# Two gate rows of an adaLN block: from wide broadcast matmuls to width-1 column matmuls, spread by DMA through DRAM

## Chip, cores, metric

One core of one Trainium2 chip. The metric is device time in microseconds (us) for one execution; medians of several runs are quoted. The record marks an execution slow when it is over 1.5% above the fastest of its kernel; all runs compared here are fast, except that two looks of one run each (marked) have no state of their own.

## The reference, cut

```python
mod = (_silu(c) @ w_mod).reshape(c.shape[0], 6, 1, -1)      # c: 1x512, w_mod: 512 x 3072
sa, ca, ga, sb, cb, gb = (mod[:, i] for i in range(6))      # six rows of 512
x = x + ga * _A_ref(_layernorm(x) * (1 + ca) + sa, ...)     # attention, 32 heads, 2048 tokens
x = x + gb * _B_ref(_layernorm(x) * (1 + cb) + sb, ...)     # gated MLP mixing over tokens
```

The block is of the adaLN kind: shift, scale and gate of each layer normalisation are rows computed from a vector `c`. `sa, ca, sb, cb` multiply tensors whose feature axis lies on the partitions, so the kernel wants them as columns (128 partitions x 4). `ga` and `gb` multiply tensors with tokens on the partitions, so it wants them as a row of 512 repeated on all 128 partitions.

## The kernel before

It runs 128 attention "units" (8 head groups x 16 token tiles) of eight slots each. Calls hung at `(unit, slot)` are issued at the start of that slot, ahead of its own matmuls. Its matmuls write to tiles in PSUM; the small pieces of work here share two PSUM buffers ("banks") named "misc", which VectorE empties.

```python
def mod_part(i, wmod, w0, mc_ps):          # columns: 16 matmuls of width 1 for one part
    for dt in range(NDT):
        for kt in range(NDT):
            nc.tensor.matmul(mc_ps[:, i * NDT + dt : i * NDT + dt + 1],
                lhsT=wmod[:, kt, w0 + dt * P : w0 + (dt + 1) * P],
                rhs=sc_bf[:, kt : kt + 1], start=(kt == 0), stop=(kt == NDT - 1))
...
def qk(u, i):                              # two width-512 matmuls and one exponential per slot
    ...
def pv(u, i):                              # eight width-129 matmuls per slot
    ...
def wo_proj(u):                            # one width-512 matmul in each of slots 4 to 7,
    ...                                    # reads oT, a DMA transpose of the attention output
...
at(8, 1, lambda: rest_w.update(lhs=mod_lhs()))   # 4 broadcasts of silu(c) to 128x128
at(9, 4, mod_cols_b)                             # sb, cb: mod_part twice
at(10, 4, lambda: mod_row(ga_rows, 2, rest_w["lhs"]))   # 4 matmuls of width 512
at(11, 4, lambda: mod_row(gb_rows, 5, rest_w["lhs"]))
...
at(it + 7, 3, lambda g=g: load_wq(g, nc.gpsimd))        # loads of the next head group
```

## Time and profile before

| | before |
|---|---|
| time, median of 3 runs | 1323.28 us (1322.88 to 1323.29) |
| TensorE share of the chain that ended last | 98% |
| plain attention unit | 8.81 us |
| unit with a gate row (four width-512 matmuls) | 9.67 us |
| unit with 32 width-1 matmuls | 9.61 us |

The lines behind the table are in the prediction. How to read it: TensorE never runs dry in the loop (busy for 57.70 of the 57.70 us from 84.6 to 142.3), so the length of a unit is the sum of what TensorE does in it, and the difference between a unit with and one without some piece of work is what that piece costs.

### The profile page before, as it was taken

How to read it: one execution, taken by the hardware profiler on the slowest of the kernel's cores; microseconds unless marked ns; L12 is line 12 of the kernel's file. 1: busy time of each engine (PE TensorE's matmuls, PEld its weight loads, DVE VectorE, ACT ScalarE, POOL GpSimd, SP SyncE). 2: the span in 40 equal slices, each digit the busy share in tenths (PEclk: the TensorE clock that was granted, in tenths of full speed). 3: DMA queues.
4: the chain of work that ended last, by engine and by line, in shares of the span. 5: the costliest groups of instructions: out<-in, count | busy, mean ns of one | idle time of the engine just before them, and what ended most of it. 6: DMA issues, size and time to landing. Idle time of an engine off the chain costs nothing.

```text
span 1321.5 us, 27879 instructions
## 1 busy us (share of the span) xinstructions
PE 1312.4 (99%) x12335; PEld 858.3 (65%) x12335; DVE 473.5 (36%) x1166; ACT 1077.8 (82%) x1061; POOL 49.4 (4%) x92
## 2 busy tenths in 40 slices
PE   9999999999999999999999999999999999999998
PEld 5666666666666666666666666666666666644445
DVE  5632222222222222222222222222222566794444
ACT  6898999999999999999999999999999999650000
POOL 1200000000000000000000000000000000120000
PEclk9999999999999999999999999999999999999999
DMA  7541022102111112111110211021101111143300
GB/s 180 141 104 33 14 49 37 37 15 51 31 23 35 32 37 37 31 35 37 33 36 14 53 37 33 18 53 21 33 14 21 25 33 30 33 116 80 69 21 26
DMA packets 148704, 58.12 MB, mean 44 GB/s; under 512 B 138368, under 2 KB 144768, under 8 KB 148576
## 3 DMA queue, kind: packets, MB, share of 16 engines
q1 hardware_dynamic: 141776, 37.65, 15.1%
q0 software_dynamic: 4208, 16.39, 4.1%
q10 hardware_dynamic: 2592, 2.23, 0.5%
q8 instruction: 98, 1.61, 0.5%
q14 instruction: 30, 0.25, 0.1%
HBM read 21.37 MB, written 2.10 MB: 18 GB/s over the span
## 4 chain that ended last, share of the span: by engine, by line
PE 98%; DMA 0%; DVE 0%; SPq 0%; issue 0%
PE o_ps L993 35%; PE s_ps L971 33%; PE misc L1025 8%; PE misc L938 8%; PE misc L1344 7%; PE s_ps L1190 2%; PE s_ps L1229 2%; PE o_ps L1365 1%; PE s_ps L1365 1%; DMA x_sb<-in_A_x_dram 0%; PE misc L1101 0%; DVE tmp L1377 0%; DVE yout L1378 0%; DVE bnst L691 0%; SPq L700 0%; SPq L745 0%
## 5 line engine op out<-in xcount | busy, mean ns | idle before, releaser
L978 ACT ACTIVATE pT<-s_ps 128x1024 bf16<-128x1024 f32 x1024 | 1044.5, 1025 | 82.9 <-PE s_ps L971 9.0
L993 PEld LDWEIGHTS <-pT 128*128 128x128 bf16 x8192 | 548.5, 98 | 241.2
L993 PE MATMUL o_ps<-v,pT 128*128 128x129 bf16 x8192 | 631.4, 220 | 0.0
L971 PE MATMUL s_ps<-qT,kT 128*128 128x512 bf16 x2048 | 609.0, 379 | 0.0
L1004 DVE RECIPROCAL rall<-o_ps 128x2 f32<-128x2 f32 x256 | 43.7, 171 | 743.8 <-PE o_ps L993 743.5
L971 PEld LDWEIGHTS <-kT 128*128 128x128 bf16 x2048 | 199.3, 98 | 118.7 <-DVE qT L920 0.5
L1025 PE MATMUL misc<-wo_g,oT 128*128 128x512 bf16 x512 | 194.0, 379 | 0.0
L938 PE MATMUL misc<-hT,wq_g 128*128 128x512 bf16 (+2 forms) x528 | 189.6, 371 | 0.0
L1005 DVE TENSOR_TENSOR onorm<-o_ps,rall 128x256 bf16<-128x256 f32 x256 | 108.7, 425 | 9.0 <-DVE rall L1004 0.3
L1344 PE MATMUL misc<-wsp,z 128*128 128x512 bf16 (+2 forms) x560 | 100.7, 336 | 0.0
L949 DVE CAST qT<-misc 128x512 bf16<-128x512 f32 x127 | 86.3, 681 | 1.8 <-PE misc L938 1.6
L1344 PEld LDWEIGHTS <-z 128*128 128x128 bf16 x560 | 50.6, 98 | 48.5
L1038 DVE TENSOR_TENSOR xacc<-misc,xacc 128x512 f32<-128x512 f32 x112 | 76.2, 680 | 0.0
L938 PEld LDWEIGHTS <-wq_g 128*128 128x128 bf16 x528 | 50.6, 98 | 1.1 <-issue 0.2
L1025 PEld LDWEIGHTS <-oT 128*128 128x128 bf16 x512 | 50.1, 98 | 0.8
L1359 DVE TENSOR_TENSOR gb<-misc,bsp_bc 128x512 bf16<-128x512 f32 (+1 forms) x28 | 18.4, 659 | 59.0 <-PE misc L1344 59.0
L1190 PE MATMUL s_ps<-win_sb,hT 128*128 128x448 bf16 x128 | 27.0, 352 | 0.0
L1200 ACT ACTIVATE z<-s_ps 128x896 bf16<-128x896 f32 x16 | 14.7, 917 | 14.9 <-PE s_ps L1190 14.9
L1229 PE MATMUL s_ps<-hT,win_sb 128*128 128x512 bf16 x112 | 24.5, 379 | 0.0
L1237 ACT ACTIVATE z1T<-s_ps 128x1024 bf16<-128x1024 f32 x14 | 14.3, 1024 | 10.0 <-PE s_ps L1229 9.1
L691 DVE BATCH_NORM_STATS2 bnst<-x_sb 128x6 f32<-128x512 bf16 x32 | 21.9, 684 | 1.5 <-DMA x_sb<-in_A_x_dram 1.0
L715 POOL DMA_DIRECT2D wq_g<-in_A_wq_dram x7 | 5.3, 753 | 420.9 <-PE misc L938 420.9
(87 smaller groups left out, 283.2 us busy)
## 6 DMA issues: line engine op xcount, KB each, us to landing
wq_g<-in_A_wq_dram POOLq DMA_DIRECT2D x7, 512.0 KB, 3.8
v<-in_A_v_cache_dram POOLq DMA_DIRECT2D x7, 512.0 KB, 7.2
wo_g<-in_A_wo_dram POOLq DMA_DIRECT2D x7, 512.0 KB, 4.7
oT<-onorm SPq DMA_TRANSPOSE x128, 2.4
wsp<-in_w_mod_dram POOLq DMA_DIRECT2D x1, 2048.0 KB, 11.7
out_dram<-yout ACTq DMA_DIRECT2D x16, 128.0 KB, 1.7
win_sb<-in_B_w_in_dram POOLq DMA_DIRECT2D x1, 1792.0 KB, 7.7
x_sb<-in_A_x_dram SPq DMA_DIRECT2D x3, 512.0 KB, 5.6
```

What stands on the lines that cost most here:

```text
L938: nc.tensor.matmul(ps[0][:, o0 : o0 + n], lhsT=wqs[g][:, dt, hh * DH : (hh + 1) * DH], rhs=hTs[ch][:, dt, c0 : c0 + n], start=(dt == 0), s ...
L949: nc.vector.tensor_copy(out=dst, in_=src)
L971: nc.tensor.matmul(s_ps[:, h * 512 : (h + 1) * 512].rearrange("p (r q) -> p r q", r=REP), lhsT=groups[g]["kT"][:, kt * P : (kt + 1) * P], ...
L978: nc.scalar.activation(out=pTs[u][:, 2 * i : 2 * i + 2, :], in_=s_ps[:].rearrange("p (k q) -> p k q", k=2), func=ACT.Exp, scale=inv_sqrt_dh,)
L993: nc.tensor.matmul(o_ps[:, hh % 2, 0 : DH + 1], lhsT=pTs[u][:, kt, hh * P : (hh + 1) * P], rhs=groups[g]["v1"][:, kt, 0 : DH + 1], start=( ...
L1004: nc.vector.reciprocal(out=rall[:, c0 : c0 + 2], in_=o_ps[:, :, DH])
L1005: nc.vector.tensor_tensor(out=onorms[u][:, hh - 1 : hh + 1, :], in0=o_ps[:, :, 0:DH], in1=rall[:, c0 : c0 + 2].unsqueeze(2).to_broadcast([ ...
L1025: nc.tensor.matmul(X_ps[:], lhsT=oTs[u][:, hh, :], rhs=groups[g]["wo"][:, hh, :], start=(hh == 0), stop=(hh == REP - 1),)
L1038: nc.vector.tensor_tensor(out=xaccs[j][:], in0=X_ps[:], in1=xaccs[j][:], op=ALU.add)
L1190: nc.tensor.matmul(ps[0][:, hf * 512 : hf * 512 + FC], lhsT=h2Ts[j // CT][:, dt, (j % CT) * P : (j % CT + 1) * P], rhs=win_sb[:, dt, FH + ...
L1229: nc.tensor.matmul(ps[0][:, k * 512 : (k + 1) * 512], lhsT=win_sb[:, dt, f * P : (f + 1) * P], rhs=h2Ts[2 * ch2 + k][:, dt, :], start=(dt ...
L1344: nc.tensor.matmul(g_ps[:, :n], lhsT=z2[:, st, f * P : (f + 1) * P], rhs=wsp[t][:, st, c0 : c0 + n], start=(st == 0), stop=(st == NT - 1 a ...
```

## The change

Its intent: the wide form computes each gate row 128 times over, once for every partition, in matmuls 512 columns wide (0.86 us for four). The narrow form computes each value once, as columns, and leaves the spreading to DMA, which has time to spare: before the change the DMA engines are busy for 7% and 23% of the two units with gate rows.

```diff
--- before.py
+++ after.py
@@ -635,6 +635,7 @@
     psum = fast.enter_context(
         tc.tile_pool(name="psum", bufs=2, space=bass.MemoryType.PSUM)
     )
+    dram = fast.enter_context(tc.tile_pool(name="dram", bufs=1, space=bass.MemoryType.DRAM))
     res = fast.enter_context(tc.tile_pool(name="res", bufs=1))
     stat = fast.enter_context(tc.tile_pool(name="stat", bufs=2))
     wspp = fast.enter_context(tc.tile_pool(name="wspp", bufs=1, side="right"))
@@ -1079,33 +1080,23 @@
         at(it + 1, 4, second)
         at(it + 2, 5, third)
 
-    def mod_lhs():
-        lhs = []
-        for kt in range(NDT):
-            lhs_bc = res.tile([P, P], BF16, name=f"lhs_bc{kt}")
-            nc.vector.tensor_scalar_mul(
-                out=lhs_bc[:], in0=ones_bf[:], scalar1=sc[:, kt : kt + 1]
-            )
-            lhs.append(lhs_bc)
-        return lhs
-
     def mod_cols_b():
         mc_ps = bank("misc")
         for i in range(2):
             mod_part(i, wmod_b, (1 + i) * D, mc_ps)
         mod_copy(3, mc_ps)
 
-    def mod_row(row_out, i, lhs):
-        mr_ps = bank("misc")
-        for kt in range(NDT):
-            nc.tensor.matmul(
-                mr_ps[:],
-                lhsT=lhs[kt][:],
-                rhs=wmod_b[:, kt, (i - 2) * D : (i - 1) * D],
-                start=(kt == 0),
-                stop=(kt == NDT - 1),
-            )
-        nc.vector.tensor_copy(out=row_out[:], in_=mr_ps[:])
+    def mod_rows():
+
+        mc_ps = bank("misc")
+        for i, row in enumerate((0, 3)):
+            mod_part(i, wmod_b, row * D, mc_ps)
+        for i, (part, rows) in enumerate(((2, ga_rows), (5, gb_rows))):
+            cols = slice(part * NDT, (part + 1) * NDT)
+            nc.vector.tensor_copy(out=modc[:, cols], in_=mc_ps[:, i * NDT : (i + 1) * NDT])
+            line = dram.tile([D], FP32, name=f"mod{part}")
+            nc.gpsimd.dma_start(out=line[:].rearrange("(dt p) -> p dt", p=P), in_=modc[:, cols])
+            nc.gpsimd.dma_start(out=rows[:], in_=line[:].partition_broadcast(P))
 
     def load_wsp(tile_, t, st):
         nc.sync.dma_start_transpose(
@@ -1146,13 +1137,10 @@
     ln1_at(1, (0, 7), (1, 2), (2, 2))
     ln1_at(2, (2, 4), (3, 1), (4, 5))
     ln1_at(3, (5, 1), (5, 5), (7, 4))
-    rest_w = {}
     at(2, 5, lambda: nc.gpsimd.dma_start(out=wmod_b, in_=wmod_dram[:, :, 2 * D : NMOD]))
     at(5, 5, lambda: nc.gpsimd.dma_start(out=win_sb[:], in_=win_dram))
-    at(8, 1, lambda: rest_w.update(lhs=mod_lhs()))
     at(9, 4, mod_cols_b)
-    at(10, 4, lambda: mod_row(ga_rows, 2, rest_w["lhs"]))
-    at(11, 4, lambda: mod_row(gb_rows, 5, rest_w["lhs"]))
+    at(10, 4, mod_rows)
 
     def set_fill(b):
 
```

## The prediction

> **What bounds the kernel now.** I read the page from the coarse parts to the fine ones: engine shares, the chain that ended last, then that chain in time around the instructions that the change touches.
>
> ```profile
> PE 1312.4 (99%) x12335; PEld 858.3 (65%) x12335; DVE 473.5 (36%) x1166; ACT 1077.8 (82%) x1061; POOL 49.4 (4%) x92
> ...
> PE 98%; DMA 0%; DVE 0%; SPq 0%; issue 0%
> PE o_ps L993 35%; PE s_ps L971 33%; PE misc L1025 8%; PE misc L938 8%; PE misc L1344 7%; PE s_ps L1190 2%; PE s_ps L1229 2%; PE o_ps L1365 1%; PE s_ps L1365 1%; DMA x_sb<-in_A_x_dram 0%; PE misc L1101 0%; DVE tmp L1377 0%; DVE yout L1378 0%; DVE bnst L691 0%; SPq L700 0%; SPq L745 0%
> ```
>
> TensorE is busy 99% of the span, and 98% of the chain is TensorE as well: almost nothing ever makes it wait. So a change pays what it takes off or puts on TensorE's own stream, and work on other engines counts only if it creates a wait that is not there today. The matmuls to be replaced (line 1101) are in the chain, at a rounded 0%. That alone says that the size is small. Closer:
>
> ```profile
> 94.63 0.78 PE misc L848 x32
> 95.41 0.45 PE s_ps L971 x2
> ```
>
> ```profile
> 104.24 0.86 PE misc L1101 x4
> ```
>
> ```profile
> 113.91 0.86 PE misc L1101 x4
> ```
>
> Columns are start, length (both us), what. Line 1101 is the two gate rows, four matmuls of width 512 each, one group in attention unit 10 and one in unit 11. Line 848 is the form that the change goes over to: 32 matmuls of width 1, here for the shift and scale columns sb and cb in unit 9, from the same weight tile. So the kernel before already holds a measurement of the new form, in the same place of the loop (slot 4 of a unit).
>
> A check by another route is the period of the loop. The first output-projection matmul of each unit starts at these times:
>
> ```profile
> 86.71 0.22 PE misc L1025
> ...
> 96.32 0.22 PE misc L1025
> ```
>
> ```profile
> 105.99 0.22 PE misc L1025
> ```
>
> ```profile
> 115.66 0.22 PE misc L1025
> ```
>
> ```profile
> 124.46 0.21 PE misc L1025
> ```
>
> ```profile
> 133.27 0.22 PE misc L1025
> ```
>
> The periods are 9.61, 9.67, 9.67, 8.80 and 8.81 us. The plain unit takes 8.81; the unit with 32 narrow matmuls takes 0.80 more, each unit with a gate row 0.86 more. These marginal costs hold any start-up or switching cost that the lengths of pieces could miss, and they agree with them within 0.02 us.
>
> [...] the line 1101 matmuls are recorded at 379 ns each, while four of them advance the chain by only 0.86 us, 215 ns each. I therefore count in chain time and periods, not in recorded durations.
>
> [...] 0.86/4 = 215 ns, and 0.78/32 = 24.4 ns. [...] a width-1 matmul needs its own 128x128 weight load, recorded at 96 ns. [...] 32 loads lie within 1.06 us before and beside the group, 33 ns apart, so several are in flight together.
>
> [...] The trace has 1.7 us for the 1 KB load of c (issued elsewhere) and 3.8 us for 512 KB of wq[...].
>
> **The change part by part.**
>
> TensorE, removed: two groups of four width-512 matmuls, 2 x 0.86 = 1.72 us of the chain. Added: 32 width-1 matmuls (two parts x four output blocks x four contraction blocks) as one group in unit 10, 0.80 us by the period of unit 9 (0.78 by piece). Net on TensorE: 0.80 - 1.72 = -0.92 us.
>
> VectorE, removed: four broadcast multiplies of 128x128 (248 ns each, 0.99 us) and two copies of 128x512 (681 ns each, 1.36 us). Added: two copies of 128x4, at 156 ns by the existing one of that shape, 0.31 us. Net -2.04 us, worth nothing: VectorE is 36% busy and no TensorE wait of this stage is put on it. The PSUM bank of the gates comes free sooner, since 0.31 us of copies stand where 0.68 us stood; also worth nothing, as TensorE did not wait for the bank.
>
> GpSimd queue, added: four DMAs. The order of instructions in the changed build puts them after the loads for head group 1 and ahead of the wq load for group 2. Each write takes 512 single FP32 elements (128 partitions x 4) to DRAM, and each read spreads 2 KB over 128 partitions, 256 KB in all. Estimates from this trace: a 512-piece load costs GpSimd 0.75 (wq) to 0.96 us (w_mod) to issue, a 128-piece broadcast 0.59 us. A landing should take 2 to 4 us for the scattered write and 2 to 6 us for the spread (512 KB of b_sp by broadcast took 5.9). A read waits in the queue for its own write to land, so one pair holds the queue some 0.9 + 3 + 0.6 = 4.5 us and both some 9 us: from 105.4, when the copies end, to about 114.4. What stands around that:
>
> ```profile
> 62.75 0.76 POOL L733 DMA_DIRECT2D wo_g<-in_A_wo_dram  x1
> 114.20 0.75 POOL L715 DMA_DIRECT2D wq_g<-in_A_wq_dram  x1 [50.69 <-PE misc L938]
> 163.05 0.20 POOL L721 MEMSET v<- 128x128 bf16 x1 [48.10 <-PE o_ps L993]
> ```
>
> The queue idles for 50.69 us before the wq load of 114.20 and 48.10 us before the next step. So the four DMAs fall into idle time. The worst case delays that wq load by a few microseconds; the first matmul that reads it starts at 269.77, and it lands in 3.8 us, so it has about 150 us to spare.
>
> Use of the rows: ga_rows is first read at 1036.2, gb_rows at 1221.3; both would be in place by about 120, more than 900 us early.
>
> Sum: 1323.28 - 0.92 = 1322.36, rounded to 1322.4 us.
>
> **The rivals.**
>
> First, narrow matmuls could run at the pace of their weight loads: 32 x 96 ns = 3.07 us instead of 0.80, making the kernel 3.07 - 1.72 = 1.35 us slower, 1324.6. For it: one full weight load per column of output. Against it: the existing group of the same form took 0.78 us, with weights from the same tile.
>
> Second, DMA trouble. The 1,024 four-byte writes and the two spreads could slow the transposes of onorm on the SP queue (2.4 us each), on which the output projection waits. Their slack is large: the projection of a unit runs two iterations after its attention product began, so a transpose issued at the end of one 8.8 us iteration is first read one and a half iterations later, some 13 us. A held-up GpSimd queue has the 150 us above. Only if the queue stood still beyond all of this would time be lost; I would expect 0 to 2 us then.
>
> Third, ScalarE takes over as the bound, and the saving is lost. It is the nearest engine: 8 exponentials of 1025 ns make 8.20 us per unit against TensorE's 8.81. But units without gate rows already run at 8.81 with TensorE gapless, so unit 11 shortened to 8.81 becomes only what its neighbours are. Effect on the time: none.
>
> Fourth, a hopeful one: the shorter VectorE list starts something earlier. With no TensorE wait on VectorE here, there is nothing to gain; the kernel stays at 1322.4.
>
> **Range and chances.** The effect is 0.07% of the time. The three runs before spread 0.41 us, almost half the effect, so I allow about 0.7 us each way: 1321.7 to 1323.1. For 2%, 26 us would have to appear or vanish. No saving of that size exists in what is removed (1.72 us of TensorE), so faster by 2% gets 0.003. Slower by 2% would need a stall that I cannot see, perhaps in the DRAM round trip: 0.007. Within 2%: 0.99.
>
> **What would show it.** In the changed trace: the 32 new width-1 matmuls as one piece of about 0.78 us near 104.2; the unit periods 9.61, 9.61, 8.81, 8.81 where they were 9.61, 9.67, 9.67, 8.80; TensorE waits no longer than before; GpSimd with four more DMA issues between about 105 and 116; the multiply by ga_rows with no idle time put on a DMA. The prediction is wrong if the new group takes over 1.7 us, if TensorE waits on line 938 near 270 or on an oT transpose after 105, or if the saving in that stretch is given back elsewhere.

Passages that this case's traces do not show are cut from it, where marked; the measured lengths beside them stay. The sum: 1323.28 - 1.72 + 0.80 = 1322.36 us, all from the trace. The 2 to 4 us for the landing of the scattered write were the estimate; the trace before has no such write, and its nearest landings are 1.7 us (1 KB of c), 2.4 (a transpose of onorm) and 3.8 (512 KB of wq).

## The result

| | before | after |
|---|---|---|
| time, median of 6 runs each | 1323.25 us (1322.82 to 1323.65) | 1322.35 us (1322.23 to 1322.66) |
| ratio | | 0.9994, 95% interval 0.9981 to 1.0007 |

Ratios here are the mean time of one kernel's fast runs over that of the other's of the same rounds, so they are not quite the ratio of the medians quoted. The interval is wider than the effect, and the verdict by the 2% rule is "same". Still, the two sets of runs do not overlap, and the trace shows where the difference lies. Predicted were 1322.4 us and a saving of 0.92; measured are 1322.35 and 0.90. That the two agree so closely is partly luck: the six runs after the change alone spread over 0.43 us.

The page of the changed kernel, engine shares and chain:

```profile
PE 1301.1 (99%) x12152; PEld 858.8 (65%) x12359; DVE 471.5 (36%) x1162; ACT 1076.7 (82%) x1061; POOL 51.8 (4%) x96
...
PE 98%; issue 1%; DVE 0%
```

PE should not be read as 11 us less busy: 12152 matmuls stand beside 12359 weight loads, so some 200 matmul records are missing from this trace, and the "issue" share of the chain is the 0.05 us holes that they leave. The times between surviving records are sound. The chain in time, changed kernel (start, length, what):

```profile
87.11 0.22 PE misc L1026
...
95.03 0.78 PE misc L849 x32
96.72 0.21 PE misc L1026
...
104.64 0.78 PE misc L849 x32
106.33 0.22 PE misc L1026
...
115.13 0.22 PE misc L1026
...
123.94 0.21 PE misc L1026
...
132.75 0.22 PE misc L1026
```

Line 1026 is the first output projection of each unit (line 1025 before), line 849 the narrow groups (848 before). The new group at 104.64 takes 0.78 us as one piece. The periods are 9.61, 9.61, 8.80, 8.81 and 8.81: unit 10 came down from 9.67 to 9.61 and unit 11 from 9.67 to 8.80. From the first to the last line it is 45.64 us, where the same stretch before (86.71 to 133.27) took 46.56: 0.92 us saved.

GpSimd's instructions in order of time, changed kernel (start, length, what, idle time before and what ended it):

```profile
106.05 0.76 POOL L1098 DMA_DIRECT2D mod<-modc  x1 [42.15 <-DVE modc L1096]
114.77 0.56 POOL L1099 DMA_DIRECT2D ga_rows<-mod  x1 [7.96 <-DMA mod<-modc]
115.32 0.76 POOL L1098 DMA_DIRECT2D mod<-modc  x1
126.33 0.55 POOL L1099 DMA_DIRECT2D gb_rows<-mod  x1 [10.25 <-DMA mod<-modc]
126.92 0.75 POOL L716 DMA_DIRECT2D wq_g<-in_A_wq_dram  x1
```

Here is the one thing that I had sized badly. The writes to DRAM, 2 KB each, held the queue 7.96 and 10.25 us after their issue, not the 3 us estimated, so the queue was held from 106 to 127 and not to 114, and the wq load for head group 2 left at 126.92 instead of 114.20. It cost nothing, and the experiments ask both why not and how far that goes.

### The profile page after: what moved, and what is told of

It reads as the page before. It is cut to its first block, busy times and chain, and to the rows that moved or that the text cites. A ratio compares the mean times of both kernels' runs of the same rounds, so it can differ in the third digit from the quotient of the medians.

```text
span 1320.9 us, 27722 instructions
## 1 busy us (share of the span) xinstructions
PE 1301.1 (99%) x12152; PEld 858.8 (65%) x12359; DVE 471.5 (36%) x1162; ACT 1076.7 (82%) x1061; POOL 51.8 (4%) x96
## 4 chain that ended last, share of the span: by engine, by line
PE 98%; issue 1%; DVE 0%
PE s_ps L972 36%; PE o_ps L994 35%; PE misc L939 7%; PE misc L1332 7%; PE misc L1026 6%; PE s_ps L1178 2%; PE s_ps L1217 2%; PE o_ps L1353 1%; PE o_ps L780 1%; PE s_ps L1353 0%; PE misc L849 0%; DVE tmp L1365 0%; DVE yout L1366 0%; PE misc L1340 0%; PE misc L826 0%
## 5 line engine op out<-in xcount | busy, mean ns | idle before, releaser
L939 PE MATMUL misc<-hT,wq_g 128*128 128x512 bf16 (+2 forms) x465 | 166.2, 370 | 0.1
L1026 PE MATMUL misc<-wo_g,oT 128*128 128x512 bf16 x386 | 146.3, 379 | 0.0
```

What stands on the lines that cost most here:

```text
L939: nc.tensor.matmul(ps[0][:, o0 : o0 + n], lhsT=wqs[g][:, dt, hh * DH : (hh + 1) * DH], rhs=hTs[ch][:, dt, c0 : c0 + n], start=(dt == 0), s ...
L1026: nc.tensor.matmul(X_ps[:], lhsT=oTs[u][:, hh, :], rhs=groups[g]["wo"][:, hh, :], start=(hh == 0), stop=(hh == REP - 1),)
```

## The experiments

Twelve kernels ran. My theory: only TensorE's own stream counts, at 0.86 us per wide group and 0.80 per narrow one, and the DMAs are hidden. The rivals: the DMAs eat part of the saving; narrow matmuls cost more than their piece shows; another engine caps the gain.

### The two halves of the change alone

`no_dma` keeps the narrow matmuls and drops the DMAs; the result is wrong.

```diff
-            line = dram.tile([D], FP32, name=f"mod{part}")
-            nc.gpsimd.dma_start(out=line[:].rearrange(...), in_=modc[:, cols])
-            nc.gpsimd.dma_start(out=rows[:], in_=line[:].partition_broadcast(P))
+            nc.gpsimd.memset(rows[:], 1.0)
```

> The narrow matmuls of the change without its four DMAs; the gate rows are set to 1.0 on GpSimd, so the result is wrong on purpose. Theory (only TensorE's stream counts, the DMAs are hidden): 1322.3 us, within 0.3 of the changed kernel's 1322.35. Rival (the DMAs cost something, so part of the saving was given back): 1321.9 or less, and then the matmuls alone would save more than the 0.92 us predicted.

Measured: 1322.33 us (1322.06 to 1322.45), ratio to before 0.9994. It is the time of the changed kernel to 0.02 us; against the kernel before in its own rounds (1323.09) the saving is 0.76, which differs from 0.90 by less than the spread of the runs.

`dma_only` keeps the wide matmuls and adds the four DMAs.

```diff
     at(11, 4, lambda: mod_row(gb_rows, 5, rest_w["lhs"]))
+    at(12, 4, extra_dma)   # the same write and spread, twice, from modc parts 3 and 4
```

> The kernel before, both row groups kept, plus the same four DMAs in unit 12 (they carry other columns of the modulation and overwrite the rows, so the result is wrong on purpose). Theory: 1323.25 us, no change, with the landing of the transposes of onorm beside the scattered writes lengthened from 2.4 us to between 4 and 9 us as in the changed kernel, still inside their slack. Rival (DMAs cost time): 1323.7 or more.

Measured: 1323.04 us (1322.92 to 1323.30) against 1323.09 for before in the same rounds, ratio 1.0. In fact the first write left at 96.1, in unit 9 and not 12, because the queue waits only for the columns it reads: the profile ends its wait of 32.54 us with the copy of those columns on VectorE (line 860). Transposes of onorm landed up to 9.3 us after issue, as expected. So the saving comes whole from the matmuls, and the DMAs neither give nor take anything that these runs can resolve. (No run takes VectorE's smaller load alone; the unit periods leave nothing for it.) The rival "DMAs eat part of it" falls.

### The price of each kind of group

`rows_x32`: 32 more wide groups, four per unit in units 12 to 19.

```diff
+    for it in range(12, 20):
+        at(it, 4, lambda: mod_row(gb_rows, 5, rest_w["lhs"], 4))   # the 4 matmuls, 4 times
```

> The kernel before plus 32 more row groups (four width-512 matmuls each), four per unit in units 12 to 19. Theory: 0.86 us per group, 27.5 us in all, so 1350.8 us. Rival (ScalarE takes over and hides part of each group): clearly under 27.5 us of growth, 20 us or less.

Measured: 1350.91 us, 27.8 over the 1323.09 of before: 0.87 per group.

`cols_x32`: the changed kernel with 32 more narrow groups in the same places.

```diff
+    for it in range(12, 20):
+        at(it, 4, extra_cols)   # mod_part for both gate parts, 4 times over: 128 matmuls
```

> The changed kernel plus 32 more groups of 32 width-1 matmuls, four groups per unit in units 12 to 19. Theory: 0.78 to 0.80 us per group, 25.0 to 25.6 us in all, so 1347.3 to 1348.0 us. Rival (the weight loads set the pace at 96 ns each): 98 us in all, so 1420 us.

Measured: 1361.74 us, 39.4 over the changed kernel: 1.23 us per group and 14 us more than the theory allows, though far from the 98 of the rival. The theory misses something. Busy time by stretch, `cols_x32` (window, its length, then busy time of TensorE, its weight loads, VectorE, ScalarE and GpSimd, granted clock, DMA share, GB/s). The granted clock is the share of TensorE's full clock rate that the trace records as given:

```profile
113.00:124.00 11.00, 11.00 (x153) 7.93 (x152) 3.58 (x9) 9.51 (x10) 1.31 (x2) 1.00 0.21 39
124.00:136.00 12.00, 10.46 (x158) 7.23 (x156) 1.35 (x4) 6.48 (x7) 1.30 (x2) 1.00 0.36 78
136.00:148.00 12.00, 12.00 (x202) 9.00 (x200) 2.55 (x7) 6.59 (x8) 0.00 (x0) 0.86 0.01 3
```

The third number from the right, the granted clock, is 1.00 in the first two windows and 0.86 in the third, while TensorE is "busy" all 12.00 us of it. (The second window, in unit 12, is another case: full clock, but TensorE busy for only 10.46 us; more on it below.) The chain in the third window shows where:

```profile
137.13 3.18 PE misc L849 x128
...
140.76 0.45 PE o_ps L994 x8
...
142.14 0.87 PE o_ps L994 x8
143.01 0.43 PE misc L1026
...
145.08 0.22 PE misc L1026
```

The 128 narrow matmuls themselves go at their usual pace (3.18 us, 24.8 ns each, against 24.4 in a group of 32). Some 1.1 us after them, ordinary matmuls take twice as long (eight of line 994 in 0.87 us, not 0.45; a projection in 0.43, not 0.22), for about 3.4 us (a mean clock of 0.86 over 12.00 us is 3.36 us at half rate); then all is as before. So in this run half clock follows a stretch packed with width-1 matmuls, although TensorE is recorded as busy throughout. The unit period confirms the size: 13.67 us from 132.51 to 146.18 (line 1026, slot 7 of two units), where 8.81 + 4 x 0.80 = 12.01 was due: 1.66 us lost per unit, in seven of the eight units, 11.6 in all. In unit 12 the clock stayed at 1.00 and stalls took 2.3 us instead (14.30 from line 939 at 122.61 to the same at 136.91). The sum, 13.9, is the 14 us that were missing.

The chain also says when the seven drops begin: about 13.65 us apart, though the runs of narrow matmuls come 13.67 apart. (The two line 972 matmuls that a drop falls into start 13.67 us apart and grow from 0.71 us in the first of the seven units to 0.80 in the last.) The drops thus do not keep step with the ends of the runs. What times them is not shown; unit 12, which was spared, also had its run broken by the stalls.

### Does it depend on how many stand in a row?

`cols_spread` puts the same 32 groups in one at a time, `cols_pairs` two at a time.

```diff
     for it in range(12, 20):
-        at(it, 4, extra_cols)             # 4 groups in a row
+        for slot in (0, 2, 4, 6):         # cols_spread: 1 group; cols_pairs: slots 0 and 4, 2 groups
+            at(it, slot, extra_cols)
```

> The same 32 extra narrow groups as in the run that came out at 1361.7 us, but one at a time in slots 0, 2, 4 and 6 of units 12 to 19. Theory of the clock (a run of some 3.1 us of narrow matmuls makes the granted clock drop to half for about 3.4 us; one group of 0.78 us doesn't): 25.0 to 25.6 us over the changed kernel, so 1347.3 to 1348 us, and full clock throughout. Rival (a group simply costs 1.23 us once there are many of them): 1361.7 us again.

> The same 32 extra narrow groups, two at a time in slots 0 and 4 of units 12 to 19 (1.56 us of narrow matmuls in a row). Theory of the clock: [...] I expect no drop and 1347.3 to 1348 us; a time between that and 1361.7 us would put the limit near this length. Rival (cost per group): 1361.7 us.

Measured: 1352.09 us (spread) and 1350.82 us (pairs), between the two theories. The unit periods settle the clock's part. In the pairs, the projection of slot 7 of successive units starts at 133.04, 145.05 and 157.06: 12.01 us each, which is 8.81 + 4 x 0.80 to the digit, and the spread version has 143.83, 155.84, 167.85 (slot 6), 12.01 again. So neither one group (0.78 us) nor two (1.58 us) in a row drop the clock here, while four (3.18 us) did in seven of eight units. The same window as above, `cols_pairs`:

```profile
136.00:148.00 12.00, 11.89 (x215) 9.17 (x216) 2.71 (x8) 8.18 (x9) 0.00 (x0) 1.00 0.07 14
```

What stays is 4.2 us (spread) and 2.9 us (pairs) over 1347.9, and both traces have them in one place, unit 12. The chain of `cols_spread` there:

```profile
127.17 0.67 PE misc L849 x21
127.83 1.15 issue
128.99 0.16 PE misc L849
```

In the middle of a group TensorE stops for 1.15 us with no wait that the profile can name, and half clock follows (0.86 on average from 124 to 136; two matmuls of line 972 take 0.85 us, not 0.43, at 130.91). ScalarE stands idle at the same moment, for 2.38 us, also with no releaser. It comes as the second scattered write to DRAM ends: GpSimd goes on behind that write at 127.76. In the pairs the same kind of stop begins earlier, at 125.82, while that write is still in flight (GpSimd goes on at 128.51).

`spread_no_dma` is `cols_spread` with the DMAs replaced by the memset of `no_dma`.

> The kernel with 32 extra narrow groups spread one per slot, now without the four DMAs (gate rows set to 1.0 on GpSimd, wrong on purpose). With the DMAs it took 1352.1 us, where 32 times the steady 0.80 us from its unit periods (12.01 against 8.81 with four groups) would give 1347.9; its trace has one stall and one stretch of half clock in unit 12, just as the second scattered write to DRAM is in flight. Theory [...]: without DMAs there is no such stall and the time is 1347.9 us, within 0.5. Rival (the narrow groups alone cause the stall and the drop of the clock in unit 12): 1352 us again.

Measured: 1348.24 us (1347.95 to 1348.54), 25.9 over `no_dma`, 0.81 per group. The stall and the drop in unit 12 are gone. Busy time by stretch, `spread_no_dma`:

```profile
124.00:136.00 12.00, 12.00 (x218) 9.17 (x216) 2.85 (x10) 8.18 (x9) 0.00 (x0) 1.00 0.07 14
```

So it takes the DMAs and a dense run of narrow matmuls together. Of the DMAs, the write is the one to suspect: when the stop of the pairs begins, the first spread has landed (issued at 115.33, 4.7 us to landing) and the second spread and the wq load are not yet issued.

My reading, which is not shown, is that the write holds up the supply of instructions. What the trace records are fetches of instructions (queue q8, pieces of 16 KB). In one window of 1 us, `cols_pairs` first, `spread_no_dma` second (count, MB, share of 16 DMA engines):

```profile
q8 instruction: 1, 0.02, 21.3%
```

```profile
q8 instruction: 1, 0.02, 5.9%
```

Both windows are 121 to 122. The shares mean 3.41 us for the fetch beside the second write (0.213 x 16) and 0.95 us without writes. The changed kernel has one such long fetch too, of 3.33 us (in the window 124 to 125), beside the second write, without losing time by it; it has no narrow matmuls there. No other fetch in the changed kernel, and none in the kernel before, took over 1.6 us. That TensorE starved for this fetch is still not shown: the stalls are only called "issue".

### How far the hidden DMAs stay hidden

`dma_x16` repeats write and spread eight times for each row.

```diff
+            for _ in range(8):
                 nc.gpsimd.dma_start(out=line[:].rearrange("(dt p) -> p dt", p=P), in_=modc[:, cols])
                 nc.gpsimd.dma_start(out=rows[:], in_=line[:].partition_broadcast(P))
```

> The changed kernel with the pair of write and spread repeated eight times per row (16 pairs). A pair should hold the GpSimd queue for 14 to 16 us (landing of the write 8 to 10, issues 1.3, landing of the spread 4.7 before the next write may start), so the queue reaches the wq load of group 2 at 330 to 365 us instead of 127, and the projection that needs it at 269 stalls for 65 to 100 us: 1387 to 1425 us. That would show the 150 us of slack to be real and finite. Rival (queued DMAs are harmless at any number): 1322.3 us.

Measured: 1400.9 us (1399.5 to 1404.9). Waits of TensorE in `dma_x16` (who waited for what: us in total, times, longest):

```profile
PE misc L939 <- DMA wq_g<-in_A_wq_dram: 74.6, 1, 74.6
```

The queue reached the wq load at 326.87, the projection had wanted it at 259.9 (334.49, when it went on, less 74.6). The profiled run took 1400.01 us, 77.7 over the changed kernel, and the stall is 74.6 of that; the rest agrees with a clock that stays low for some time after it: 0.50 from 270 to 330, in the stall, and 0.83 on average from 330 to 360 (two matmuls of line 972 take 0.85 us, not 0.43, at 335.10). The queue's slack is real and ends where said, with one correction: group 2's first projection is at 260.97 in the kernel before, one unit earlier than the 269.77 that my prediction took, so there were some 143 us to spare and not 150.

### Why the small write lands late

`write16` writes each partition's four values as one 16-byte piece (the row's order is then wrong); `write_hw` issues the unchanged write from the SP queue.

```diff
-            nc.gpsimd.dma_start(out=line[:].rearrange("(dt p) -> p dt", p=P), in_=modc[:, cols])
+            nc.gpsimd.dma_start(out=line[:].rearrange("(p dt) -> p dt", p=P), in_=modc[:, cols])  # write16
+            nc.sync.dma_start(out=line[:].rearrange("(dt p) -> p dt", p=P), in_=modc[:, cols])    # write_hw
```

> The changed kernel with the rows written to DRAM as one 16-byte piece per partition (128 pieces) in place of four 4-byte pieces (512); the order of the row is then wrong on purpose. If the landing grows with the number of small pieces written to DRAM, it falls from 8.4 to 10.5 us to 2 to 4 us; if it is a fixed cost of a write to DRAM from this queue, it stays at 8 to 10 us. The time stays at 1322.3 us in both cases.

> The changed kernel with the two scattered writes issued from the SP queue instead of GpSimd's, still as 512 pieces of 4 bytes. If the slow landing comes from the many small pieces written to DRAM, it stays at 8 to 10 us; if it comes from GpSimd's own way of issuing, it falls to 2 to 4 us. Time 1322.3 us in both cases.

Measured: 1322.52 and 1322.13 us, no change in time, as expected. GpSimd's instructions in `write16`:

```profile
107.93 0.55 POOL L1099 DMA_DIRECT2D ga_rows<-mod  x1 [1.43 <-DMA mod<-modc]
...
113.81 0.54 POOL L1099 DMA_DIRECT2D gb_rows<-mod  x1 [4.80 <-DMA mod<-modc]
114.42 0.76 POOL L716 DMA_DIRECT2D wq_g<-in_A_wq_dram  x1
```

The waits for the write fell from 7.96 and 10.25 us to 1.43 and 4.80 with the same bytes in a quarter of the pieces; the wq load leaves at 114.42, as early as before the change. With the SP queue the write was issued at 105.48 and the spread that waits for it began at 114.40, 8.9 us later, so GpSimd's way of issuing is not the cause. (The landing times listed for that run, 5.4 and 5.9 us, are those of the two spreads; none is listed for the writes.) The changed kernel and `write16` differ by 512 pieces of 4 bytes against 128 of 16; their number and their size changed together, and each version was looked at once. What in the write path takes the time is not shown.

### A version that beats both

The lesson of the result is that only TensorE's stream is worth money, and VectorE is 36% busy. `fold` lets VectorE add up the four contraction blocks of each part beforehand (multiply by the per-partition scalar and add, FP32, the last rounded to bf16). Then one width-512 matmul with a block of ones sums over partitions and repeats the row on all of them, and four width-1 matmuls make the sb or cb columns. No DMA is needed. In the trace of `fold` the four VectorE instructions of a part take 0.47, 0.75, 0.74 and 0.75 us, 10.8 us for the four parts.

```diff
+    def fold(acc, w0, kt):          # one of 4 per part, in slots 1, 2, 5, 6 of units 8 to 11
+        ...scalar_tensor_tensor(out=fold_bf[:] if kt == NDT - 1 else acc[:],
+            in0=wmod_b[:, kt, w0 : w0 + D], scalar=sc[:, kt : kt + 1], in1=acc[:], op0=mult, op1=add)
+    def fold_row(rows):
+        nc.tensor.matmul(mr_ps[:], lhsT=ones_bf[:], rhs=fold_bf[:], start=True, stop=True)
+        nc.vector.tensor_copy(out=rows[:], in_=mr_ps[:])
-    at(9, 4, mod_cols_b)
-    at(10, 4, mod_rows)
+        at(9 + k, 0, last)          # the TensorE part of part k, slot 0 of the next unit
```

> A candidate to beat both: VectorE sums the four contraction blocks of each part first (16 instructions of 128x512, one per slot in units 8 to 11), so TensorE needs one width-512 matmul per gate row (0.215 us each) and four width-1 matmuls each for the sb and cb columns (0.1 us each); no DMAs. Theory (only TensorE's stream counts): 0.63 us where the kernel before has 1.72 + 0.80 = 2.52 us, so 1.89 us under before and 1.0 us under the changed kernel: 1321.3 us. Rival (VectorE, delayed by some 11 us of new work, holds up copies that TensorE waits for): 1322.3 us or more, with TensorE waits on VectorE in units 8 to 12.

Measured: 1322.20 us (1321.86 to 1322.82), correct, half of the hoped saving lost. The chain of `fold`, at the first TensorE part:

```profile
90.33 0.42 DVE onorm L1005
90.75 0.61 DVE xacc L1036
91.36 0.04 issue
91.40 0.38 PE misc L938
```

The chain leaves TensorE for VectorE. The two banks named "misc" take turns; the extra bank in slot 0 means that the projection of line 938 gets the bank that line 1036 empties, behind two other VectorE instructions. The attention matmuls ahead of it end at about 91.1 (eight in 0.45 us from 90.67), so it waits some 0.25 us. This happens at both column parts; at the two gate rows the wait is some 0.15 us. In all, units 8 to 12 take 1.47 us more than five plain units, where 0.63 was due. `fold2` moves the TensorE parts to slot 4, the columns of sb and cb together.

```diff
-        at(9 + k, 0, last)
+    at(10, 4, fold_cols)            # sb and cb, eight width-1 matmuls
+    at(11, 4, lambda: fold_row(ga_rows))
+    at(12, 4, lambda: fold_row(gb_rows))
```

> The fold with VectorE's partial sums, its TensorE parts moved from slot 0 to slot 4 (both column parts at once in unit 10, the gate rows in units 11 and 12). In the first version the next projection waited some 0.25 us in each of four places for a PSUM bank that VectorE frees late (its copy follows the normalisation of the attention output), and 0.9 us of the expected 1.9 was lost. Theory: in slot 4 the bank is free in time, so 1321.3 to 1321.5 us. Rival (VectorE's extra work itself slows the loop): 1322.2 us again.

Measured: 1321.49 us (1321.37 to 1322.12), correct, ratio to before 0.9988. The chain of `fold2` at the columns:

```profile
103.62 0.18 PE misc L1102 x8
...
104.25 0.45 PE o_ps L993 x8
...
104.72 0.38 PE misc L1025
```

No VectorE piece is left in it, yet the waits are not gone. The projection starts 0.23 us after the last attention matmul where 0.06 is usual, just as VectorE ends line 949 (103.98 to 104.66), which empties the other bank. The projections of slot 3 in units 10 to 13 start at 103.40, 112.58, 121.76 and 130.94: 9.18 us each, 0.37 over a plain unit, for pieces of 0.18 and 0.22 us. So the new pieces cost 1.11 us, where 0.63 was worked out and `fold` had 1.47: some 0.16 us of wait stays at each of three places. The better slot and the one place less both helped; no run separates them. The rival, that VectorE's added work slows the loop as such, finds no support: VectorE was idle for 2.00 us before it began the steps that end in line 949. The median is 1.58 us under before (1323.07 in its rounds) and 0.86 under the changed kernel (0.68 if each is taken against before in its own rounds), the fastest of the three versions.

## Why the prediction was right

The bound: right. TensorE's stream sets the end, and nothing outside it moved the time (`no_dma`, `dma_only`).

TensorE's sum: right, term by term. A wide group was put at 0.86 us and cost 0.87 in bulk; a narrow one at 0.80 and cost 0.80 to 0.81 wherever no more than two stood in a row and no scattered write was in flight. The sum of -0.92 us was measured as -0.90 in the medians and -0.92 in the unit periods.

VectorE's relief: right that it is worth nothing; its busy time fell from 473.5 to 471.5 us, the 2.04 worked out.

GpSimd's queue: the mechanism was right and a size was off. The landing of the scattered write was put at 2 to 4 us and waits of 7.96 and 10.25 us were measured, so the wq load left 12.7 us later where "a few" were said, the last of the four issues came at 126.33 and not by 116, and the rows were in place by 131 and not 120. The first reader of that load was put one unit late (269.77 for 260.97). All of it falls inside the slack.

The rivals: weight loads did not set the pace (0.78 us, not 3.07). ScalarE did not take over (unit 11 ran in 8.80 us). The fourth, an earlier start, did not come. The second was closer than I had thought: among the transposes of onorm issued from 100 to 131, landing took 2.4 us as a median and 3.9 at most before, and 4.7 and 9.0 after, out of some 13 us of slack. Why they landed later is not shown. What I had not foreseen at all is that half clock can follow narrow matmuls (`cols_x32`, 0.86 on average over 12 us); the change stays clear of it with one group at a time (1.00 from 104 to 116).

## What to carry to other kernels

When one engine's stream is the whole chain, price a change by the length of the loop's periods with and without the piece concerned, from the trace that you already have; here it gave the result to 0.05 us, closer than single runs agree. Ask of every piece of that stream whether an idle engine can do a part of it ahead (`fold2`), and check which buffer the new piece makes its neighbour wait for. Narrow matmuls were cheap one group at a time (0.80 us for 32); 128 of them, packed into 3.18 us, cost a further 1.7 us afterwards through the clock in seven of eight units, which no busy time shows.
